# RWKV attention and a gated MLP on one core: decay, k and r packed into three blocks of 128 features, with heads 6 and 7 gathered by moves inside SBUF

## The chip, the core and the metric

The kernel runs on one core of one Trainium2 chip. The core has a matrix engine (PE, with its weight loads on PEld), three engines for vectors (DVE, ACT, POOL), and queues that issue DMAs; in the kernel before, all of them go out from the queue of the Sync engine (SPq). The metric is device time in microseconds of one launch. "Span" is the time from the first to the last instruction in a profiled execution.

## The reference, cut to what matters

Four sequences, 8 heads, 768 tokens, 48 features per head. First a linear attention with a decay per feature, then a gated MLP whose gate mixes the tokens:

```python
for t in range(S):                                   # S = 768, per (b, h), D = 48
    cur = np.einsum('bhd,bhe->bhde', u[None] * kt, vt)
    y[:, :, t] = np.einsum('bhd,bhde->bhe', rt, state + cur)
    state = wt[:, :, :, None] * state + np.einsum('bhd,bhe->bhde', kt, vt)
...
h = gelu(x @ w_in)                                   # x is y as (b, t, 384); d_ff = 1024
u, v = h[..., :512], h[..., 512:]
v_n = (v - mu) / np.sqrt(var + 1e-06) * g_ln
v_s = np.einsum('ts,bsd->btd', w_sg, v_n) + b_sg[None, :, None]
out = x + (u * v_s) @ w_out
```

## The kernel before

**Tiling.** The 768 tokens of a sequence are six chunks of 128 (`C`), so there are 24 chunks. In a chunk the decays are turned into running products, and the attention becomes matmuls: the scores of the chunk's own tokens (`scores`, L486), the product with the state that the earlier chunks left (`outputs`, L548), the product of the masked scores with v (L563), and the update of the state (`state`: transposes of k, L500, and k with v, L510). The MLP works on halves of a sequence (three chunks): `v_piece` per chunk, then four `u_piece`, four `gate_piece` and three `out_piece` per half. Every MLP product is three matmuls (L632, L633, L634), since both operands are split in a high and a low part.

**Layout of decay, k and r.** Eight heads of 48 features lie in four blocks (`NP`), two heads per block: one in partitions 0 to 47, one in 64 to 111. Partitions 48 to 63 and 112 to 127 are padding. So a tile of w, k or r is 128 partitions by 4 x 128 tokens (512 columns).

**Per chunk.** `decays` scans w backwards (L408, 516 columns) and forwards (L413); L415 and L436 multiply r and k by the results; `range_check` (L424) squares the products for a check of their size; `chunk_pc` copies the four last columns into a tile of its own, by which `decayed` scales the state (L531 on ACT, L533 elsewhere). `own_weights` makes the weight of each token for itself: in the first 8 chunks (`OWN_PE`) r times k (L446) and four matmuls with `u_col` (L450), later from a second copy of k and r, laid out by tokens (L458, L460, L463). L471 or L473 puts these weights on a diagonal, and L490 copies the scores in below it.

**What sets the order.** [...] Each piece of work is a generator that yields `Op`s with a cost for each engine that may run it, what they come after, and which buffers they take and free. `Plan.run` plays all generators against these costs and ranks and picks engine and place, so each engine and the DMA queue get a fixed order. The ranks come from tables of numbers (`LEAD`, `FIRST`, `PIECE`, `WEIGHT`). An engine works its list in order, and waits at the first instruction whose inputs aren't there.

**Weights.** `f64_weight` loads a weight matrix as 64-bit numbers and makes a high and a low part: four DVE instructions (L761, L763, L766, L768), one on ACT (L785), three matmuls (L772 to L774). The six blocks of `w_in` must be ready before the first `v_piece` and `u_piece`. Three of them use buffers of `vn`, three those of `xT`.

**Moves.** Heads 3 and 7 leave `outputs` in a tile of their own and are put into the padding of x by six small DMAs per chunk or half (`move`, L600).

## Time and profile before

| | us |
|---|---|
| median of 3 runs | 404.07 (403.16 to 404.13) |
| the profiled execution's own time | 402.04 |
| its span | 400.3 |
| PE busy | 378.3 (95% of the span) |
| DVE busy | 294.2 (73%) |
| ACT busy | 200.2 (50%) |
| POOL busy | 94.2 (24%) |

A busy time is the union of an engine's instructions. A row of a group gives line, engine, operation, the tile written and the tiles read, shapes and count, then busy time and mean duration, then the idle time in front and what ended it. A row of a timeline gives start, duration, engine, line, operation and count. A row of a table of stages gives, for each stage, its length and each engine's busy time (with the number of instructions), the clock granted to PE and the share of the DMA engines.

### The profile page before, as it was taken

The page shows a single profiled execution, that of the slowest core. Times are in us where ns is not written, and L with a number is a line of the kernel's source. Part 1 is how long each engine was busy: PE and PEld are TensorE (multiplying, and loading weights), DVE is VectorE, ACT ScalarE, POOL GpSimd, SP SyncE. Part 2 cuts the span into 40 slices and gives each one's busy share as a digit, 9 for nine tenths or more (in the row PEclk, how much of TensorE's full clock was granted, in tenths as well). Part 3 has the DMA queues.
Part 4 walks back from the last instruction along what each step waited for, and adds up shares of the span by engine and source line. Part 5 has one row for each costly group of instructions (what it writes and reads, how often), then busy time and mean ns, then how long its engine had stood idle before and what let it go on. Part 6 is the DMA issues. An engine that isn't in the chain of part 4 may idle for free. (4 is left out here: it accounts for less than half of the span.)

```text
span 400.3 us, 7881 instructions
## 1 busy us (share of the span) xinstructions
PE 378.3 (95%) x2964; PEld 329.8 (82%) x2964; DVE 294.2 (73%) x573; ACT 200.2 (50%) x534; POOL 94.2 (24%) x127
## 2 busy tenths in 40 slices
PE   2799889999999999999999999999999999999993
PEld 2666567889898988988899988979899789999993
DVE  7699989889989999998798489956653355543251
ACT  3566575685555447746454246563272576502010
POOL 3003551123073543444550003124100002100000
PEclk9999899999999999999999999999999999999999
DMA  8918667343134634335422316222133520100101
GB/s 281 355 42 250 188 220 241 129 135 105 46 131 160 221 118 144 98 122 196 155 88 77 105 65 211 60 88 96 61 106 111 186 95 2 39 22 0 61 0 66
DMA packets 23933, 48.82 MB, mean 122 GB/s; under 512 B 4048, under 2 KB 13008, under 8 KB 23888
## 3 DMA queue, kind: packets, MB, share of 16 engines
q1 hardware_dynamic: 23888, 48.25, 36.6%
q8 instruction: 25, 0.41, 0.4%
q14 instruction: 20, 0.16, 0.1%
HBM read 42.34 MB, written 4.72 MB: 118 GB/s over the span
## 5 line engine op out<-in xcount | busy, mean ns | idle before, releaser
L632 PE MATMUL m_ps<-wsgh,vn 128*128 128x384 f32 x192 | 67.7, 353 | 0.8 <-DVE g L714 0.8
L634 PE MATMUL m_ps<-wsgh,vn 128*128 128x384 f32 x192 | 64.7, 337 | 0.0
L633 PE MATMUL m_ps<-wsgl,vn 128*128 128x384 f32 x192 | 64.6, 337 | 0.0
L473 POOL TENSOR_SCALAR_AFFINE_SELECT a<-own 128x512 f32<-128x512 f32 x25 | 20.3, 815 | 94.9 <-PE y_ps L563 44.9
L632 PEld LDWEIGHTS m_ps<-wsgh,vn 128*128 128x128 f32 x192 | 36.1, 188 | 5.5 <-issue 2.9
L712 ACT CAST g<-m_ps 128x384 fp32r<-128x384 f32 x32 | 15.1, 479 | 50.1 <-DVE m_ps L710 50.0
L490 DVE COPY_PREDICATED a<-mask,a_ps 128x512 f32<-128x512 uint8 x48 | 34.4, 730 | 4.5 <-POOL a L473 2.5
L663 POOL TENSOR_TENSOR st<-st,mhalf 128x1 f32<-128x1 f32 x24 | 15.3, 640 | 90.9 <-DVE st L661 87.7
L633 PEld LDWEIGHTS m_ps<-wsgl,vn 128*128 128x128 f32 x192 | 36.2, 188 | 0.4
L634 PEld LDWEIGHTS m_ps<-wsgh,vn 128*128 128x128 f32 x192 | 36.1, 188 | 0.0
L708 DVE SCALAR_TENSOR_TENSOR m_ps<-m_ps,g_ln,b_bc 128x384 f32<-128x384 f32 x32 | 19.7, 622 | 21.5 <-PE m_ps L634 21.4
L632 PE MATMUL m_ps<-g,wouth 128*128 128x384 f32 x96 | 33.7, 351 | 0.4 <-DVE g L714 0.4
L632 PE MATMUL m_ps<-xT,winh 128*128 128x384 f32 x96 | 33.4, 348 | 0.0
L408 DVE TENSOR_TENSOR_SCAN W<-W,D 128x516 f32<-128x516 f32 x24 | 32.0, 1332 | 1.6 <-DMA W<-in_wpad 1.6
L634 PE MATMUL m_ps<-xT,winl 128*128 128x384 f32 x96 | 32.4, 337 | 0.0
L633 PE MATMUL m_ps<-xT,winh 128*128 128x384 f32 x96 | 32.4, 337 | 0.0
L633 PE MATMUL m_ps<-g,wouth 128*128 128x384 f32 x96 | 32.4, 337 | 0.0
L634 PE MATMUL m_ps<-g,woutl 128*128 128x384 f32 x96 | 32.4, 337 | 0.0
L413 DVE TENSOR_TENSOR_SCAN W<-W,D 128x516 f32<-128x516 f32 x24 | 31.4, 1308 | 0.1
L471 ACT ACTIVATE a<-ident,own 128x128 f32<-128x128 f32 x92 | 29.1, 393 | 3.9 <-DVE own L463 3.8
L632 PE MATMUL m_ps<-winh,xT 128*128 128x512 f32 x72 | 30.5, 424 | 0.0
L424 ACT ACTIVATE junk<-W 128x1032 f32<-128x1032 f32 x24 | 25.6, 1066 | 9.8 <-DVE W L413 6.8
(142 smaller groups left out, 856.5 us busy)
## 6 DMA issues: line engine op xcount, KB each, us to landing
KR<-in_kr SPq DMA_DIRECT2D x24, 512.0 KB, 3.5
W<-in_wpad SPq DMA_DIRECT2D x24, 258.5 KB, 2.9
RK<-in_ktok SPq DMA_DIRECT2D x16, 384.0 KB, 3.2
vtok<-in_vtok SPq DMA_DIRECT2D x24, 192.0 KB, 3.1
out<-o SPq DMA_DIRECT2D x24, 192.0 KB, 1.9
KR<-in_w_in SPq DMA_DIRECT2D x6, 512.0 KB, 4.1
u<-in_w_sgT SPq DMA_DIRECT2D x12, 192.0 KB, 3.6
vn<-in_w_in SPq DMA_DIRECT2D x3, 512.0 KB, 7.3
```

Of the source, the lines that this page charges most:

```text
L408: nc.vector.tensor_tensor_scan(Suf[:, WL - 1:0:-1], W[:, WL - 1:0:-1], D1[:, WL - 1:0:-1], 0.0, ALU.mult, ALU.add)
L413: nc.vector.tensor_tensor_scan(W[:, 0:WL - 1], W[:, 0:WL - 1], D2[:, 0:WL - 1], 0.0, ALU.mult, ALU.add)
L424: nc.scalar.activation(junk.rearrange("p (a x) -> p a x", a=2), both, AF.Square, accum_out=chk[:, n:n + 1])
L471: nc.scalar.activation(a[:, p], ident, AF.Copy, scale=own.tile[:, 2 * p + j:2 * p + j + 1])
L473: nc.gpsimd.affine_select(a, own.tile[:, j:H:2].unsqueeze(2).broadcast_to([128, NP, C]), pattern=[[0, NP], [1, C]], compare_op=ALU.is_equa ...
L490: nc.vector.copy_predicated(x.a[j].tile, mask, a_ps.tile[j])
L632: nc.tensor.matmul(ps, lh, rh, start=(i == 0), stop=False)
L633: nc.tensor.matmul(ps, lh, rl, start=False, stop=False)
L634: nc.tensor.matmul(ps, ll, rh, start=False, stop=(i == n - 1))
L663: nc.gpsimd.tensor_tensor(rstd, var, c.mhalf, ALU.pow)
L708: nc.vector.scalar_tensor_tensor(ps, ps, c.g[:, d:d + 1], c.b_bc[:, ts], ALU.mult, ALU.add)
L712: nc.scalar.copy(gh, ps)
```

## The change

**Layout.** w, k and r of all eight heads are packed into three blocks (`NB`) of 128 full partitions. Heads 0 to 5 keep their 48 partitions in each half of a block; heads 6 and 7 are cut into three pieces of 16 features, which fill partitions 48 to 63 and 112 to 127. Loads, scans, multiplications and the check so run over three quarters of the columns, and the transposes and the matmuls with `u_col` are three instead of four. For the scores and the product with the state, heads 6 and 7 are needed in a block of their own: `gather` moves them, after the multiplications, by six DMAs per chunk from the padding rows of the three blocks to a fourth block of the same tile. The copy of the last decays now lies in that tile and moves along. Matmuls on k and r read 48 partitions per head instead of 64. The copy of the transposed k (`kt`) becomes three copies that sort the heads.

**Order.** The planner gets a later time for an `Op` that takes several buffers, lets the two diagonals, the three copies of y and the small DMAs be ordered apart from each other, can issue moves from SPq or from ACT's queue, charges PE for turning from large to small matmuls, and has new ranks. The `w_in` blocks all go through buffers of `vn` and wait for less. `u_col` is laid out by the caller and loaded in one DMA. The weights for the own token come from PE in the first 5 chunks instead of 8. KR has four buffers instead of three.

**Order on PE up to the first piece of the MLP.** PE's rows just before the first `v_piece`, which starts at L632. `KR_0_82` is chunk 3 here, the x tile's block is that of chunk 0. Before:

```order
L563 MATMUL y_ps_1_129<-a_0_97,vtok_0_87 64x128 x4
L772 MATMUL m_ps_0_131<-xT_367,ident 128x512
...
L548 MATMUL y_ps_1_129<-KR_0_82,S_0_103 64x128
L500 MATMUL k_ps_0_127<-ident,KR_0_82 128x128 x4
L486 MATMUL a_ps_0_125<-KR_0_82 128x128
...
L621 MATMUL m_ps_0_132<-x_0_105,ident 128x384
L622 MATMUL m_ps_0_132<-xT_506,minus 128x384
L510 MATMUL k_ps_0_127<-vtok_0_85,kt_0_100 64x48 x8
L450 MATMUL m_ps_0_130<-u_col,RK_0_89 128x8 x4
L632 MATMUL m_ps_0_131<-winh,xT_506 128x512
```

With the change (L534 is the transposes, L548 k with v, L601 the masked scores with v, L663 the split of x, L674 the first MLP matmul; `KR_0_84` is chunk 2):

```order
L586 MATMUL y_ps_1_126<-KR_0_83,S_0_100 64x128
L534 MATMUL k_ps_0_124<-ident,KR_0_84 128x128 x3
L601 MATMUL y_ps_0_125<-a_0_95,vtok_0_87 64x128 x4
L601 MATMUL y_ps_1_126<-a_0_96,vtok_0_87 64x128 x4
L548 MATMUL k_ps_0_124<-vtok_0_88,kt_0_97 64x48 x8
L808 MATMUL m_ps_0_128<-vn_253,ident 128x512
...
L663 MATMUL m_ps_0_129<-x_0_102,ident 128x384
L664 MATMUL m_ps_0_129<-xT_416,minus 128x384
L808 MATMUL m_ps_0_127<-vn_277,ident 128x512
...
L674 MATMUL m_ps_0_128<-winh,xT_416 128x512
```

The first `v_piece` stood behind the scores of chunk 3; it now stands ahead of the scores of chunk 2, right behind the last block of `w_in`.

**Order on the DMA queue of SP.** The loads of the weights, before (`vn` and `xT` take `w_in`, the third and later rows of KR and W are chunks 2 and on):

```order
L384 DMA KR_0_84<-in_kr 128x1024
L392 DMA vtok_0_87<-in_vtok 128x384
L756 DMA vn_173<-in_w_in 128x1024
L756 DMA vn_177<-in_w_in 128x1024
L812 DMA u_col<-in_u 48x4x1
L756 DMA vn_183<-in_w_in 128x1024
```

and with the change, from the first loads to the first gathers (L469, the other half of whose rows go out from ACT's queue):

```order
L847 DMA u_col<-in_ucol 128x24
L399 DMA W_0_81<-in_wpad 128x388
L407 DMA KR_0_83<-in_kr 128x3x256
L415 DMA vtok_0_86<-in_vtok 128x384
L791 DMA vn_170<-in_w_in 128x1024
...
L407 DMA KR_0_85<-in_kr 128x3x256
L469 DMA KR_0_82<-KR_0_82 16x256 x3
L399 DMA W_0_80<-in_wpad 128x388
L791 DMA vn_241<-in_w_in 128x1024
```

The first `w_in` block now comes after the loads of two chunks instead of three, and three gathers of chunk 0 stand ahead of the third load of W. In the whole program 91 of the 144 gathers and 49 of the 72 moves of y are issued by SP, 53 and 23 by ACT.

The core of the diff:

```diff
...
+NB = KT
 Q = C + 1
-WL = NP * Q + 1
+WL = NB * Q + 1
+KW = 2 * C + 4
...
-LEAD = (2.78, 2.05, 2.47, 2.9)
-FIRST = {"v": -1.57, "u": 4.03, "gate": 5.24, "out": 7.56}
-PIECE = {"v": -0.45, "u": 3.56, "gate": 5.0, "out": 7.56}
-WEIGHT = {"v": -8.15, "u": -9.0, "sg0": 4.48, "sg1": 3.78, "out": 4.95, "g": -1.62}
-
-OWN_PE = 8
-COLD = 20.0
+LEAD = (2.81, 2.14, 2.13, 2.02)
+FIRST = {"v": -1.35, "u": 4.47, "gate": 2.25, "out": 7.29}
+PIECE = {"v": -0.3, "u": 4.01, "gate": 4.96, "out": 7.68}
+WEIGHT = {"v": -4.16, "u": -2.73, "sg0": 2.61, "sg1": -1.74, "out": 3.69, "g": 0.54}
+
+BIAS = {"DVE": 0.05, "POOL": 0.05}
+MOVE = {"SP": 0.53, "ACT": 0.55}
+
+ON_PE = {"own": 5, "x": 6, "w": 6}
+FIRST_LOADS = {(0, "load_w"): -20.0, (0, "load_kr"): -19.0, (1, "load_w"): -17.0, (1, "load_kr"): -16.0,
+               (0, "load_v"): -15.0}
+COLD = 15.0
...
-    def since(self):
-        return min(t for t, _ in self.free)
+    def since(self, n):
+        return sorted(t for t, _ in self.free)[n - 1]
...
+    def cost(self, op, e, t):
+
+        c = op.on[e]
+        if e == "PE":
+            c = (2 * c if t < COLD else c) + (0.09 if op.small and not self.small else 0.0)
+        return c
...
-            p[2] = op.seen
+            if not op.apart:
+                p[2] = op.seen
...
-    s_w = slots("W", 2, [2 * 521])
-    s_kr = slots("KR", 3, [2, NP * C])
+    s_w = slots("W", 2, [2 * 393])
+    s_kr = slots("KR", 4, [NP, KW])
...
-    nc.gpsimd.memset(u_col, 0.0)
     for _, t in s_S2.free:
+        nc.gpsimd.memset(t, 0.0)
+    for _, t in s_kr.free:
+        nc.gpsimd.memset(t[:, NB], 0.0)
+    for _, t in s_kt.free:
         nc.gpsimd.memset(t, 0.0)
...
+    def move_dma(kb, after):
+        return Op(MOVE, kb=kb, after=after, apart=True)
...
-        ch[n].W, ch[n].Suf = (ch[n].w.tile[:, i * 520:(i + 1) * 520] for i in range(2))
+        ch[n].W, ch[n].Suf = (ch[n].w.tile[:, i * 392:i * 392 + 390] for i in range(2))
...
+        nc.sync.dma_start(ch[n].KR[:, 0:NB, 0:2 * C], kr[b, g])
...
-        yield Op({"DVE": 1.15}, after=[x.e_W], done=x.e_suf, two=True)
+        yield Op({"DVE": 0.88}, after=[x.e_W], done=x.e_suf, two=True)
...
-        yield Op({"DVE": 1.15}, done=x.e_pre, two=True)
+        yield Op({"DVE": 0.88}, done=x.e_pre, two=True)
         nc.vector.tensor_tensor_scan(W[:, 0:WL - 1], W[:, 0:WL - 1], D2[:, 0:WL - 1], 0.0, ALU.mult, ALU.add)
-        op = yield Op({"DVE": 0.61, "POOL": 1.25}, after=[x.e_KR, *x.own], done=x.e_r, two=True)
-        engine[op.e].tensor_tensor(cols(x.KR[:, 1]), cols(x.KR[:, 1]), blocks(W, 0), ALU.mult)
+        op = yield Op({"DVE": 0.48, "POOL": 1.05}, after=[x.e_KR, *x.own], done=x.e_r, two=True)
+        r = x.KR[:, 0:NB, C:2 * C]
+        engine[op.e].tensor_tensor(r, r, blocks(W, 0), ALU.mult)
...
+        copy(op.e, x.KR[:, 0:NB, 2 * C], x.Suf[:, 1:WL - 1:Q])
...
+        op = yield Op({"DVE": 0.48, "POOL": 1.05}, after=[x.e_KR, x.e_suf, *x.own], done=x.e_k, two=True)
+        k = x.KR[:, 0:NB, 0:C]
+        engine[op.e].tensor_tensor(k, k, blocks(x.Suf, 2), ALU.mult)
...
+    def gather(n):
+
+        x = ch[n]
+        w = 2 * C + (steps[n][1] > 0)
+        for j in range(2):
+            for i in range(NB):
+                op = yield move_dma(16, [x.e_k, x.e_r, *([x.e_pc] if steps[n][1] else [])])
+                issue[op.e].dma_start(x.KR[64 * j + 16 * i:64 * j + 16 * i + 16, NB, 0:w],
+                                      x.KR[64 * j + D:64 * j + 64, i, 0:w])
+        x.e_km.t = op.seen
...
-            op = yield Op({"DVE": 0.6, "POOL": 1.25}, after=[x.e_KR], take=[s_rk], done=x.e_own, two=True)
...
-            t = rk.tile.rearrange("p a b -> p (a b)")[:, 0:NP * C]
-            engine[op.e].tensor_tensor(t, x.KR[:, 0], x.KR[:, 1], ALU.mult)
-            op = yield Op({"PE": 0.35}, after=[e_uc], take=[m_m], free=[rk])
+            t = rk.tile[:, 0].rearrange("p (b t) -> p b t", t=C)
+            engine[op.e].tensor_tensor(t, x.KR[:, 0:NB, 0:C], x.KR[:, 0:NB, C:2 * C], ALU.mult)
+            op = yield Op({"PE": 0.75}, small=True, after=[e_uc], take=[m_m], free=[rk])
             m, = op.got
-            for p in range(NP):
-                nc.tensor.matmul(m.tile[:, 0:H], t[:, p * C:(p + 1) * C], u_col[:, p], start=(p == 0),
-                                 stop=(p == NP - 1))
+            for i in range(NB):
+                nc.tensor.matmul(m.tile[:, 0:H], t[:, i], u_col[:, i], start=(i == 0), stop=(i == NB - 1))
...
         for j in range(2):
-            op = yield Op({"POOL": 0.95, "ACT": 1.2}, take=[s_a], done=(x.e_A0, x.e_A1)[j], free=[own] if j else [])
+            op = yield Op({"POOL": 0.95, "ACT": 1.2}, take=[s_a], done=(x.e_A0, x.e_A1)[j], free=[own], apart=True)
...
-        op = yield Op({"PE": 1.09}, after=[x.e_k, x.e_r], take=[m_a])
+        op = yield Op({"PE": 1.06}, small=True, after=[x.e_km], take=[m_a])
...
-                nc.tensor.matmul(a_ps.tile[j][:, p], x.KR[64 * j:64 * j + 64, 0, p * C:(p + 1) * C],
-                                 x.KR[64 * j:64 * j + 64, 1, p * C:(p + 1) * C], start=True, stop=True)
+                nc.tensor.matmul(a_ps.tile[j][:, p], x.KR[64 * j:64 * j + D, p, 0:C],
+                                 x.KR[64 * j:64 * j + D, p, C:2 * C], start=True, stop=True)
...
-        for p in range(NP):
-            nc.tensor.transpose(kt_ps.tile[:, p], x.KR[:, 0, p * C:(p + 1) * C], ident)
-        op = yield Op({"ACT": 0.5, "DVE": 0.61}, take=[s_kt], free=[kt_ps])
+        for i in range(NB):
+            nc.tensor.transpose(kt_ps.tile[:, i], x.KR[:, i, 0:C], ident)
+        op = yield Op({"ACT": 0.72, "DVE": 0.7}, take=[s_kt], free=[kt_ps])
         kt, = op.got
-        copy(op.e, kt.tile, kt_ps.tile)
-        op = yield Op({"PE": 0.6}, after=[x.e_V], take=[m_s], free=[kt])
+        halves_ = lambda t: t.rearrange("p b (j x) -> p b j x", x=64)
+        copy(op.e, halves_(kt.tile[:, 0:NB])[:, :, :, 0:D], halves_(kt_ps.tile[:, 0:NB])[:, :, :, 0:D])
+        for j in range(2):
+            copy(op.e, kt.tile[:, NB, 64 * j:64 * j + D].rearrange("p (i e) -> p i e", e=16),
+                 kt_ps.tile[:, 0:NB, 64 * j + D:64 * j + 64])
+        op = yield Op({"PE": 0.6}, small=True, after=[x.e_V], take=[m_s], free=[kt])
...
-        op = yield Op({"DVE": 0.3, "POOL": 0.6, "ACT": 1.0}, after=[before.e_S1, x.e_pc], take=[s_S2], done=x.e_S2,
+        op = yield Op({"DVE": 0.3, "POOL": 0.6, "ACT": 1.0}, after=[before.e_S1, x.e_km], take=[s_S2], done=x.e_S2,
...
             engine[op.e].tensor_tensor(x.S2.tile[:, :, 0:D], before.S1.tile,
-                                       x.pc.tile.unsqueeze(2).broadcast_to([128, NP, D]), ALU.mult)
+                                       x.KR[:, :, 2 * C:2 * C + 1].broadcast_to([128, NP, D]), ALU.mult)
         before.S1.done(op.seen)
-        x.pc.done(op.seen)
+        x.kr.done(op.seen)
...
-                nc.tensor.matmul(y.tile[j][64 * c_:64 * c_ + 64, q, 0:C], x.S2.tile[64 * j:64 * j + 64, p],
-                                 x.KR[64 * j:64 * j + 64, 1, p * C:(p + 1) * C], start=(q == 0), stop=False,
+                nc.tensor.matmul(y.tile[j][64 * c_:64 * c_ + 64, q, 0:C], x.S2.tile[64 * j:64 * j + D, p],
+                                 x.KR[64 * j:64 * j + D, p, C:2 * C], start=(q == 0), stop=False,
...
-                op = yield dma(10, after=[ch[h_.n + g].e_y for g in range(g0, g1)])
+                op = yield move_dma(10, [ch[h_.n + g].e_y for g in range(g0, g1)])
                 x, y3 = h_.x.tile, h_.y3.tile
-                nc.sync.dma_start(x[64 * j + D:64 * j + 64, i, ts], y3[64 * j + 16 * i:64 * j + 16 * i + 16, ts])
+                issue[op.e].dma_start(x[64 * j + D:64 * j + 64, i, ts], y3[64 * j + 16 * i:64 * j + 16 * i + 16, ts])
...
-        for j in range(2):
-            op = yield dma(1)
-            nc.sync.dma_start(u_col.rearrange("p a b -> p (a b)")[64 * j:64 * j + D, j:NP * H:10],
-                              u.rearrange("(p j) d -> j d p", j=2)[j])
-        e_uc.t = op.seen
+        yield dma(16, done=e_uc)
+        nc.sync.dma_start(u_col, ucol)
...
-            plan.add(r, f64_weight(*w[1:], e_win[n0][k], r, [s_vn, s_vn] if n0 else [s_xt],
-                                   [ch[0].e_KR] if n0 else [ch[1].e_k]))
...
-_INS = ["wpad", "kr", "vtok", "ktok", "vt", "u", "w_in", "g_ln", "w_sgT", "b_sg", "w_out"]
+KROWS = [h * D + e for i in range(NB) for j in range(2)
+         for h, e0, n in ((2 * i + j, 0, D), (6 + j, 16 * i, 16)) for e in range(e0, e0 + n)]
...
+    cut = lambda a: a.transpose(0, 1, 3, 2).reshape(B, DM, NC, C)[:, KROWS].reshape(B, NB, 128, NC, C).transpose(
+        0, 3, 2, 1, 4)
+    wpad = np.zeros((B, NC, 128, WL), np.float32)
+    wpad[..., 0:NB * Q].reshape(B, NC, 128, NB, Q)[..., 1:] = cut(w)
+    kr = np.stack([cut(k), cut(r)], axis=4)
+
+    ucol = np.zeros((DM, H), np.float32)
+    for h in range(H):
+        ucol[h * D:(h + 1) * D, h] = u[h]
...
```

More of the change, by code (lines that the diff above doesn't have):

```diff
@@ L427, in chunk_pc @@
         x = ch[n]
[L428 to L429 removed]
+        op = yield Op({"ACT": 0.13, "POOL": 0.38}, after=[x.e_suf, x.e_KR], done=x.e_pc)
         x.w.done(op.seen)
[L431 removed]
+        copy(op.e, x.KR[:, 0:NB, 2 * C], x.Suf[:, 1:WL - 1:Q])
     def decayed_k(n):
         x = ch[n]
[L435 removed]
@@ L572, in outputs @@
         copy(op.e, half.y3.tile[:, cs], y1[:, 1])
[L573 to L579 removed]
+        x.e_y.t = max(seen, op.seen)
     halves = {}
```

163 lines of the change are left out of this document (78 added, 85 removed).

## The prediction

> **What bounds the kernel now.** The page first: who is busy, and when.
>
> ```profile
> span 400.3 us, 7881 instructions
> ...
> PE 378.3 (95%) x2964; PEld 329.8 (82%) x2964; DVE 294.2 (73%) x573; ACT 200.2 (50%) x534; POOL 94.2 (24%) x127
> ...
> PE   2799889999999999999999999999999999999993
> ...
> DVE  7699989889989999998798489956653355543251
> ```
>
> PE is busy 378.3 of 400.3 us, so 22.0 are to be had from its idle time, and the rest only by taking work off it. The slices show two stages: an early one in which PE has gaps and DVE is as full as PE, and a long one in which PE is full. The table of stages separates them:
>
> ```profile
> 0.00:10.00 10.00, 2.93 (x27) 2.46 (x29) 7.31 (x13) 3.68 (x8) 3.14 (x19) 1.00 0.80 282
> 10.00:20.00 10.00, 7.64 (x33) 6.15 (x32) 6.48 (x13) 5.90 (x19) 0.64 (x1) 1.00 0.91 355
> 20.00:40.00 20.00, 18.88 (x195) 13.22 (x194) 20.00 (x36) 13.56 (x41) 3.64 (x4) 1.00 0.48 146
> 40.00:49.50 9.50, 7.53 (x66) 5.23 (x64) 9.50 (x14) 4.94 (x16) 5.36 (x5) 0.82 0.59 187
> 49.50:80.00 30.50, 28.75 (x264) 22.44 (x264) 26.45 (x53) 20.14 (x54) 8.39 (x13) 1.00 0.62 196
> 80.00:320.00 240.00, 239.13 (x1987) 209.90 (x1986) 189.25 (x372) 126.58 (x338) 68.46 (x77) 1.00 0.37 120
> ...
> 380.00:400.30 20.30, 13.43 (x76) 12.79 (x74) 7.64 (x14) 1.92 (x4) 0.00 (x0) 0.97 0.10 33
> ```
>
> Up to 49.5, where the first `v_piece` starts, PE is idle for 12.5 us (7.07 + 2.36 + 1.12 + 1.97), and DVE has no gap from 20 on: there DVE and the loads set the pace. From 49.5 to 380 PE is idle for 2.6 (1.75 + 0.87), and 6.9 are the tail. What PE waited for:
>
> ```profile
> PE k_ps L500 <- DVE KR L436: 6.4, 1, 6.4
> PE m_ps L450 <- DMA u_col<-in_u: 2.4, 1, 2.4
> PE y_ps L548 <- ACT S L531: 2.0, 1, 2.0
> ```
>
> The first two are the start and the late `u_col`; the third is one gap at 40.8. Behind that gap PE also runs slowly:
>
> ```profile
> 24.21 0.66 PE L500 MATMUL k_ps<-ident,KR 128*128 128x128 f32 x4
> 24.80 1.16 PE L486 MATMUL a_ps<-KR 64*128 64x128 f32 x16
> 25.89 1.06 PE L450 MATMUL m_ps<-u_col,RK 128*128 128x8 f32 x8
> 26.88 0.67 PE L510 MATMUL k_ps<-vtok,kt 128*64 128x48 f32 x16
> 27.48 0.67 PE L548 MATMUL y_ps<-KR,S 64*64 64x128 f32 x16
> ...
> 42.74 1.11 PE L548 MATMUL y_ps<-KR,S 64*64 64x128 f32 x16 [1.96 <-ACT S L531]
> ...
> 44.51 2.08 PE L486 MATMUL a_ps<-KR 64*128 64x128 f32 x16
> ...
> 50.43 1.09 PE L563 MATMUL y_ps<-a,vtok 128*64 128x128 f32 x16
> ```
>
> The scores take 2.08 us instead of 1.16, the product with the state 1.11 instead of 0.67; the granted clock of that stage is 0.82, so 0.18 x 9.5 = 1.7 us of PE time are lost beside the 2.0 of the gap. The Trainium skill ("TensorE: Matmul & The Clock Gate", Part 1) has PE at half clock until some 3.4 us of sustained work; 1.7 us lost at half clock are 3.4 us, so the trace agrees. It also warns only of idle gaps over about 3.4 us, while here a gap of 2.0 was enough; by the page a short new wait would cost its own length alone, by the trace about twice that.
>
> **The change, part by part.** I sum up to the first MLP matmul and from there on.
>
> *DVE before the first `v_piece`.* The forms of DVE up to 39.6 and its busy time from its first scan to the end of the last `w_in` conversion:
>
> ```profile
> L413 DVE TENSOR_TENSOR_SCAN W<-W,D 128x516 f32<-128x516 f32 x4 | 4.9, 1226 | 0.0
> L490 DVE COPY_PREDICATED a<-mask,a_ps 128x512 f32<-128x512 uint8 x6 | 4.3, 722 | 2.5 <-POOL a L473 2.5
> L446 DVE TENSOR_TENSOR RK<-KR 128x512 f32<-128x512 f32 x5 | 3.7, 745 | 0.0
> L436 DVE TENSOR_TENSOR KR<-KR,W 128x512 f32<-128x512 f32 x3 | 2.0, 680 | 0.0
> L761 DVE TENSOR_SCALAR vn<-vn 128x512 int32<-128x512 int32 x3 | 1.3, 423 | 1.0 <-DMA vn<-in_w_in 1.0
> ```
> ```profile
> 3.68:39.51 35.83, 28.97 (x249) 21.64 (x250) 32.31 (x57) 21.37 (x62) 4.39 (x6) 1.00 0.69 240
> ```
>
> DVE needs 32.3 us for its list up to there, and idles 3.5. In the new list scans go from seven to six and to three quarters of the columns (7 x 1.23 to 6 x 0.92: -3.1), the products for the own token from five to two (3.7 to 1.1: -2.6), the k and r products from five to four (3.4 to 2.0: -1.4), the masked copies from six to four (-1.4); an added kt copy in three pieces, three small copies and one cast, less small ones, come to about +1.4 (an estimate by columns). That leaves 25.2. From 3.7 it ends at 28.9 without a wait and at 32.4 with the 3.5 us of before. I take 30: with the sizes of the issue rows below, cut by a quarter for W and KR, the first `w_in` block has landed after 1.9 MB instead of 3.1, which at the 355 GB/s of stage 10 to 20 is 3.5 us earlier.
>
> *PE before the first `v_piece`.* Two pieces of work that weren't shown yet, a block of `w_in` (39.20 to 40.79, 1.6 us) and the split of x (56.83 to 57.92, 1.1 us):
>
> ```profile
> 39.20 1.13 PE L772 MATMUL m_ps<-xT,ident 128*128 128x512 f32 x2
> ...
> 40.40 0.39 PE L774 MATMUL m_ps<-winl,same 128*128 128x512 f32 x1
> ...
> 56.83 0.91 PE L621 MATMUL m_ps<-x,ident 128*128 128x384 f32 x2 [0.98 <-DMA x<-y]
> 57.37 0.55 PE L622 MATMUL m_ps<-xT,minus 128*128 128x384 f32 x1
> ```
>
> The third `w_in` block is converted after 13 us of DVE's list (by the same durations), at 17, and the scores of chunk 0 stand behind it on PE. From there to L674 PE has two scores, two own (three quarters of 1.06), two transposes (three quarters of 0.66), two k with v, one state and two masked products, three blocks of `w_in` and one split: 2.3 + 1.6 + 1.0 + 1.3 + 0.7 + 2.2 + 4.8 + 1.1, with 1 us for the slow clock at their start and 1.5 for turns between kinds (estimates) 17.5. So **34.5**, later than DVE's 30; not below 32 (nothing waits and the clock is up), not above 40 (before's two DVE waits and one gap with its slow clock).
>
> *The rest.* Before:
>
> ```profile
> 49.50:400.30 350.80, 341.31 (x2651) 302.74 (x2650) 250.86 (x501) 172.15 (x455) 81.43 (x98) 1.00 0.33 108
> 49.50:400.30 350.80, 2.10 (x18) 2.20 (x17) 1.00 0.33 108
> 49.50:400.30 350.80, 9.75 (x64) 7.72 (x64) 1.00 0.33 108
> ```
>
> PE has 341.3 us of work there, 2.1 of it L450 and 9.75 L500 (second and third row). The new order leaves work of chunks 2 and 3 for later that was done by 49.5: two scores, two state and one masked product, one k with v, 2.3 + 1.3 + 1.1 + 0.7 = 5.4, and one group of transposes, 0.5. The transposes are three instead of four: a quarter of 17 x 0.61, -2.6 (between 0.42 and 0.66 us per group by PEld and PE: -1.8 to -2.8). Own: two groups of three, 1.6 instead of 2.1. So 344.1.
>
> *Gathers.* No row shows one; the nearest are the six moves of y, of the same 16 partitions:
>
> ```profile
> 40.02 0.51 SPq L600 DMA_DIRECT2D x<-y  x1
> ...
> KR<-in_kr SPq DMA_DIRECT2D x24, 512.0 KB, 3.5
> W<-in_wpad SPq DMA_DIRECT2D x24, 258.5 KB, 2.9
> ...
> vtok<-in_vtok SPq DMA_DIRECT2D x24, 192.0 KB, 3.1
> ...
> vn<-in_w_in SPq DMA_DIRECT2D x3, 512.0 KB, 7.3
> x<-y SPq DMA_DIRECT2D x36, 8.0 KB, 3.1
> ```
>
> Three issues on a queue and the landing: 1.5 + 3.1 = 4.6 us from the last product to the scores, 6.2 where one queue issues all. The Trainium skill ("DMA: Bandwidth & Descriptors", Anatomy of one DMA) gives about 2.0 us of fixed cost, by which it were 3.5 us; the row decides. The wait stands in front of PE's scores, and behind them on PE all MLP work. I cost it at nothing after chunk 1, since DVE's list runs a chunk ahead of PE and MLP matmuls stand between; without that cover it is 4.6 per chunk. On SP the loads of W and RK are queued behind gathers, three or more issues of 0.5 each; these loads are a chunk early. On ACT 76 issues of 0.5, 39 us, fit beside its 200. The third wait of before (L531 on ACT) goes mostly: four such instructions are left of 40.
>
> *Idle after the start.* 2.6 before; I take 3: chunks 2 to 5 now run beside MLP work, which covers PE, but have less lead. Below: 0.5. Above: 12, three gaps like that at 40.8 with their slow clock (3.7 each). Tail: 6.9, the last matmuls are in the same order.
>
> *Sum.* 34.5 + 344.1 + 3 + 6.9 = 388.5 of span, 11.8 less than 400.3. The profiled execution's own time is 402.04, 2.0 under the median of 404.07; I take the difference from the median: **392.3**.
>
> **The rivals.**
>
> 1. *PE never waits.* v at 32, 0.5 idle: 383.5, so 387.3. For it: DVE's list is 7 us shorter, and stage 80 to 320 has 0.9 us of gaps. Against: PE gets to the scores by way of DVE, DMA and DVE again. Chance 0.25.
> 2. *DVE stays the bound up to chunk 5.* It has the masked copies, weights of `w_sg` and the first v pieces at once; PE reaches them earlier than DVE. v at 36 and 9 us of gaps: 396, so 399.8. For it: DVE 26.45 of 30.5 from 49.5 to 80. Chance 0.15.
> 3. *The gathers take the place of the waits, slower.* 24 chunks each wait for six small DMAs in front of the scores. It decides from 11.8 / 24 = 0.5 us uncovered per chunk; with 0.8 it is 388.5 + 19.2 = 407.7 of span, 411.5. For it: 4.6 us where there were 0.2. Against: the lead of about a chunk. Chance 0.08.
> 4. *Matmuls on 48 partitions don't run in pairs.* Pairs show in eight state products at 0.67 us, while four transposes take 0.66. Without them 0.65 x 20 more, 405.3. The Trainium skill ("TensorEngine Tiling (Array Packing)", When to Use Tiling) has a contraction of up to 64 in the 64-row mode; no run here shows 48. Chance 0.01.
> 5. *It gives all back.* 404, no difference: 0.03.
>
> **How the numbers follow.** The forecast has 0.48. Its own range is 386 to 399. The range for 8 in 10 takes in rival 1 and most of rival 2: 384 to 401. A difference under 0.3%, 1.2 us, can't be told from none. Faster: 0.48 + 0.25 + 0.15 = 0.88; same 0.03; slower 0.09.
>
> **What would show it.** The first MLP matmul (L674) near 34.5; PE busy under 374; the waits of PE with L520 on DMA KR at nearly nothing; no stage after 20 us with a granted clock under 0.95; scores at 1.16 per 16. Wrong: L674 after 40, a wait of L520 for KR of more than 5 us in all, or PE busy above 378.

## The result, and the profile after

The changed kernel takes **417.97 us** (median of 4 runs, 415.15 to 419.01) beside 403.62 for the kernel before (402.79 to 404.13): a ratio of 1.035, with a 95% interval of 1.029 to 1.040. It is slower. Forecast were 392.3.

The page of the changed kernel, its busy times, two engines and the clock in 40 slices, and the chain of waits by engine:

```profile
span 415.7 us, 8089 instructions
...
PE 383.6 (92%) x2910; PEld 333.9 (80%) x2910; DVE 279.8 (67%) x608; ACT 185.9 (45%) x505; POOL 88.8 (21%) x135
...
PE   2879869899999599997999999999999999999993
...
PEclk9969967999999779997999999999999999999998
...
PE 69%; DMA 11%; DVE 9%; SPq 4%; ACT 3%; issue 2%; POOL 1%; ACTq 1%; DVEq 0%; POOLq 0%
```

DVE and ACT have less to do, as the layout promised, and so has PE (2910 matmuls instead of 2964); yet PE is busy for 383.6 us, 5.3 more than before. The slices say why: at several places up to the middle of the run PE has a gap and, in the same slice or the next, a lower granted clock (the digits 5 to 8 of `PE`, 6 and 7 of `PEclk`). In the chain DMA has 11% and SPq 4%. (Before, DMA had 1%, but there the chain is followed through only a fifth of the span.)

The table of stages, cut where the first `v_piece` starts (L674, at 37.65), at 200, and at the tail:

```profile
0.00:37.60 37.60, 25.82 (x182) 18.25 (x183) 29.11 (x59) 17.26 (x48) 11.91 (x32) 0.91 0.73 234
37.60:200.00 162.40, 148.84 (x1191) 125.31 (x1191) 130.28 (x281) 83.48 (x233) 52.41 (x65) 0.91 0.44 136
200.00:395.40 195.40, 195.40 (x1468) 177.82 (x1468) 112.75 (x256) 83.23 (x222) 24.46 (x38) 1.00 0.26 82
395.40:415.70 20.30, 13.50 (x74) 12.54 (x72) 7.68 (x14) 1.93 (x4) 0.00 (x0) 0.94 0.10 34
```

The start did get shorter: L674 comes at 37.65 instead of 49.55. All of that and more is given back between 37.6 and 200, where PE idles for 13.6 us (162.40 - 148.84) at a mean clock of 0.91; from 200 on it never waits until the tail. What it waited for in that stretch (total, times, longest):

```profile
PE m_ps L674 <- DVE g L756: 4.2, 1, 4.2
PE k_ps L548 <- ACT kt L283: 3.0, 1, 3.0
PE y_ps L601 <- DVE st L703: 2.8, 1, 2.8
PE k_ps L534 <- DVE st L699: 2.0, 1, 2.0
PE m_ps L663 <- ACT v L697: 1.3, 1, 1.3
```

No row has PE waiting for a gather (`DMA KR<-KR`): the scores (L520) find their fourth block there. The five gaps lie in front of other work, and no two have the same name. Two that follow each other closely, of 2.0 and 2.8 us, followed back. First SP's queue, then the chain of waits, then PE, then DVE:

```profile
43.84 3.37 SPq L469 DMA_DIRECT2D KR<-KR  x5
47.38 0.46 SPq L399 DMA_DIRECT2D W<-in_wpad  x1
47.94 0.61 SPq L407 DMA_DIRECT2D KR<-in_kr  x1
48.60 1.18 SPq L838 DMA_DIRECT2D u<-in_w_sgT  x2
```
```profile
48.60 4.71 DMA u<-in_w_sgT
...
53.33 0.51 ACT wsgh L283
...
54.39 0.56 DVE wsgl L842
54.95 0.92 DVE vn L716
55.87 0.64 DVE a L524
```
```profile
49.83 0.67 PE L586 MATMUL y_ps<-KR,S 48*64 48x128 f32 x16
52.51 0.52 PE L534 MATMUL k_ps<-ident,KR 128*128 128x128 f32 x3 [2.01 <-DVE st L699]
53.12 0.66 PE L601 MATMUL y_ps<-a,vtok 128*64 128x128 f32 x8
56.56 1.12 PE L601 MATMUL y_ps<-a,vtok 128*64 128x128 f32 x8 [2.79 <-DVE st L703]
...
60.34 2.08 PE L520 MATMUL a_ps<-KR 48*128 48x128 f32 x16
```
```profile
48.84 0.36 DVE L571 TENSOR_TENSOR S<-S,KR 128x192 f32<-128x192 f32 x1 [1.74 <-DMA KR<-KR]
...
50.22 1.23 DVE L430 TENSOR_TENSOR_SCAN W<-W,D 128x387 f32<-128x387 f32 x1 [0.95 <-DMA W<-in_wpad]
...
52.01 0.35 DVE L558 TENSOR_TENSOR S<-k_ps,S 128x192 f32<-128x192 f32 x1
```

Five gathers hold SP for 3.4 us; the loads of W, KR and `w_sgT` (the weights that mix the tokens) stand behind them. The gap of 2.8 comes from `w_sgT`: it lands at 53.3; ACT's conversion, next in its list, has waited for it, and DVE's list waits for ACT; the masked copy (L524) is last of all. The gap of 2.0 in front of the transposes (L534) has ended before that. They write the one `k_ps` tile, which L558 has to read first, and DVE is late with L558 because its list has waited 1.74 us for a gather's landing (L571 scales the state by the moved decays) and 0.95 us for W, whose load stood behind the five gathers. After both gaps the scores take 2.08 us instead of 1.16. The gap of 3.0, which ends at 192.28, goes back to SP as well: from 170.1 to 179.4 SP issues four moves and eight gathers, with two loads between them; the RK load behind them goes out at 180.1 and lands at 185.1, and DVE's list and then ACT's copy of kt come late by it. The experiments ask whether the gathers do this, or the order, and by what.

### The profile page after: what moved, and what is told of

The parts are those of the page before. It is cut to its first block, busy times and chain, and to the rows that moved or that the text cites. A ratio compares the mean times of both kernels' runs of the same rounds, so it can differ in the third digit from the quotient of the medians.

```text
span 415.7 us, 8089 instructions
## 1 busy us (share of the span) xinstructions
PE 383.6 (92%) x2910; PEld 333.9 (80%) x2910; DVE 279.8 (67%) x608; ACT 185.9 (45%) x505; POOL 88.8 (21%) x135
## 4 chain that ended last, share of the span: by engine, by line
PE 69%; DMA 11%; DVE 9%; SPq 4%; ACT 3%; issue 2%; POOL 1%; ACTq 1%; DVEq 0%; POOLq 0%
PE m_ps L674 19%; PE m_ps L675 17%; PE m_ps L676 17%; PE a_ps L520 5%; PE y_ps L601 4%; DMA RK<-in_ktok 2%; PE k_ps L548 2%; DMA KR<-in_kr 2%; DMA x<-y 2%; DMA vn<-in_w_in 2%; PE y_ps L586 2%; SPq L469 2%; DMA u<-in_w_sgT 1%; PE k_ps L534 1%; DVE W L430 1%
## 5 line engine op out<-in xcount | busy, mean ns | idle before, releaser
L674 PE MATMUL m_ps<-wsgh,vn 128*128 128x384 f32 x192 | 70.7, 368 | 4.3 <-DVE g L756 4.2
L675 PE MATMUL m_ps<-wsgl,vn 128*128 128x384 f32 x192 | 66.8, 348 | 0.0
L676 PE MATMUL m_ps<-wsgh,vn 128*128 128x384 f32 x192 | 66.5, 346 | 0.0
L674 PEld LDWEIGHTS m_ps<-wsgh,vn 128*128 128x128 f32 x192 | 37.5, 195 | 9.4 <-DVE g L756 4.9
L754 ACT CAST g<-m_ps 128x384 fp32r<-128x384 f32 x32 | 15.3, 483 | 54.9 <-DVE m_ps L752 53.3
L675 PEld LDWEIGHTS m_ps<-wsgl,vn 128*128 128x128 f32 x192 | 37.7, 196 | 0.4
L676 PEld LDWEIGHTS m_ps<-wsgh,vn 128*128 128x128 f32 x192 | 37.5, 195 | 0.0
L524 DVE COPY_PREDICATED a<-mask,a_ps 128x512 f32<-128x512 uint8 x48 | 34.2, 726 | 3.8 <-PE a_ps L520 3.8
L674 PE MATMUL m_ps<-xT,winh 128*128 128x384 f32 x96 | 34.2, 356 | 0.0
L674 PE MATMUL m_ps<-g,wouth 128*128 128x384 f32 x96 | 33.3, 347 | 0.4 <-DVE g L756 0.4
L520 PEld LDWEIGHTS a_ps<-KR 48*128 48x128 f32 x384 | 25.7, 204 | 6.5 <-issue 6.0
L674 PE MATMUL m_ps<-winh,xT 128*128 128x512 f32 x72 | 30.8, 428 | 0.0
L601 PE MATMUL y_ps<-a,vtok 128*64 128x128 f32 x384 | 28.2, 290 | 2.9 <-DVE st L703 2.8
L520 PE MATMUL a_ps<-KR 48*128 48x128 f32 x384 | 30.6, 304 | 0.0
L447 ACT ACTIVATE junk<-W 128x774 f32<-128x774 f32 x24 | 20.4, 852 | 22.8 <-DVE W L435 16.1
```

The costliest lines, as they stand in the source:

```text
L447: nc.scalar.activation(junk.rearrange("p (a x) -> p a x", a=2), both, AF.Square, accum_out=chk[:, n:n + 1])
L520: nc.tensor.matmul(a_ps.tile[j][:, p], x.KR[64 * j:64 * j + D, p, 0:C], x.KR[64 * j:64 * j + D, p, C:2 * C], start=True, stop=True)
L524: nc.vector.copy_predicated(x.a[j].tile, mask, a_ps.tile[j])
L601: nc.tensor.matmul(y.tile[j][64 * c_:64 * c_ + 64, q, 0:C], x.V[:, h * D:h * D + 64], x.a[j].tile[:, p], start=(g == 0 and q == 0), stop=( ...
L674: nc.tensor.matmul(ps, lh, rh, start=(i == 0), stop=False)
L675: nc.tensor.matmul(ps, lh, rl, start=False, stop=False)
```

## The experiments

Theory A: the gathers cost by being issued, in queues that work in order. Theory B: the new order makes the gaps. Theory C: the way from the products through the gathers to the scores is too long. The kernel before, run beside each group of experiments, took 403.0 to 404.1 us; a ratio is always to the runs beside it.

### What the gathers cost (e1, e2, e3, e4)

**e1**, the gathers left out, the order of all else kept (heads 6 and 7 are missing from its result):

```diff
-                issue[op.e].dma_start(x.KR[64 * j + 16 * i:64 * j + 16 * i + 16, NB, 0:w],
-                                      x.KR[64 * j + D:64 * j + 64, i, 0:w])
```

> The order of the changed kernel on every engine, but the 144 gathers are not issued (the fourth block stays zero, so heads 6 and 7 are left out of the result; every other instruction is there). Theory A (the gathers, issued in order by SP and ACT, hold up the loads and the ACT work behind them): 388 to 400 us, PE idle under 25 us, granted clock 0.98 or more. Theory B (the new order itself, with its small lead of the chunks, makes the gaps, whatever the gathers do): 412 to 420 us, the same gaps between 50 and 200 us. Theory C (the landing time of a gather in front of scores and decayed state is what PE waits for) expects what A expects here; the next run tells A from C.

**397.41 us** (395.16 to 398.45), ratio 0.985 (0.980 to 0.990): the gathers cost 20.6 us. Its stages, cut at its first `v_piece`, at 180 and at the tail:

```profile
0.00:38.50 38.50, 26.30 (x183) 18.45 (x184) 28.87 (x60) 18.10 (x49) 12.79 (x32) 0.87 0.70 223
38.50:180.00 141.50, 136.68 (x1189) 116.65 (x1188) 127.49 (x277) 82.62 (x232) 52.96 (x65) 0.99 0.47 146
180.00:376.10 196.10, 196.10 (x1471) 178.44 (x1470) 114.50 (x260) 83.72 (x224) 23.51 (x39) 1.00 0.26 78
376.10:396.40 20.30, 13.20 (x72) 12.23 (x71) 7.36 (x14) 1.92 (x4) 0.00 (x0) 0.96 0.10 34
```

From the first `v_piece` on, the same matmuls keep PE busy for 346.0 us (136.68 + 196.10 + 13.20) and for 357.7 with gathers (148.84 + 195.40 + 13.50): 11.8 us are slow clock. Before the tail PE idles for 4.8 instead of 13.6: 8.7 us are waits. The changed kernel has 0.9 less at the start and 0.3 less idle time in the tail, and that is the whole difference of the spans, 19.3.

The slow clock can be seen directly. These are the stretches in which the granted clock was 0.50: all three of the changed kernel between the first `v_piece` and the tail, the one of e1 there, and the one of the kernel before behind its gap at 40.8:

```profile
54.70:68.35 13.65, 11.79 (x74) 8.30 (x76) 9.33 (x20) 4.65 (x12) 3.23 (x5) 0.50 0.61 189
140.05:150.25 10.20, 9.23 (x39) 8.47 (x40) 8.44 (x16) 3.61 (x13) 4.66 (x4) 0.50 0.31 90
191.25:198.05 6.80, 5.77 (x43) 5.35 (x44) 6.39 (x16) 3.09 (x11) 3.36 (x3) 0.50 0.30 99
```
```profile
74.00:77.35 3.35, 3.35 (x9) 2.41 (x8) 3.35 (x7) 2.41 (x6) 0.73 (x1) 0.50 0.31 79
```
```profile
44.20:47.55 3.35, 3.35 (x22) 2.52 (x19) 3.35 (x4) 1.09 (x3) 2.24 (x2) 0.50 0.44 90
```

In the changed kernel PE works 26.8 us at half clock (11.79 + 9.23 + 5.77), of which about half, 13.4, is lost; in e1 it is 1.7. The difference, 11.7, is nearly all of the 11.8. A gap of 2.0 us (before) or 2.2 (e1) was followed by 3.4 us of slow clock, one of 3.0 by 6.8, one of 4.2 by 10.2, and the pair of 2.0 and 2.8 by 13.6.

**e2**, the same order and the full result, but two DMAs a chunk in place of six, each from 16 partitions of three blocks to 48 partitions (the copy of kt follows the new order of the rows):

```diff
+            issue[op.e].dma_start(x.KR[64 * j:64 * j + D, NB, 0:w],
+                                  x.KR[64 * j + D:64 * j + 64, 0:NB, 0:w])
```

> The same order again and the whole result, but the six gathers of a chunk go out as two DMAs of 48 rows each, at the place of the third and the sixth; the rows of the fourth block are then in the order (feature, block), and the kt copy follows. 96 issues less on SP and ACT, the landing in front of the scores stays. Theory A: a good part of the loss comes back, 395 to 408 us, with RK and w_sgT loads issued earlier than in the changed kernel. Theory C: no gain, 414 to 421 us. Theory B: 412 to 420 us.

**400.52 us** (399.51 to 401.28), ratio 0.993 (0.990 to 0.996): 17.4 of the 20.6 us come back. The views of the gathers' line in the changed kernel and in e2 give their landings (least, median, most):

```profile
DMA to landing us min/median/max: 1.7/2.2/6.2
```
```profile
DMA to landing us min/median/max: 2.1/2.5/7.4
```

A gather of e2 lands later, not sooner, so it isn't the landing of the single DMA that costs. The way to the scores has become shorter by issues all the same, so e2 alone doesn't rule out theory C.

**e3** is e2 with the planner making an order of its own:

> Two gathers a chunk as in the run before, but the planner knows of it and makes its own order. Theory A: 392 to 406 us. Theory B: the order is much like that of the changed kernel, so the gaps stay: 410 to 420 us. Theory C: 412 to 420 us.

**416.88 us** (415.61 to 419.02). The same DMAs and the same work in another order: 16.4 us. Theory A alone doesn't account for this.

**e4**, the order alone: the layout of before (`NB = NP`, scans of 516 columns, four blocks, three KR buffers, no gathers) with the new rules and ranks.

> The new planner's rules, ranks and u in columns loaded whole, but the layout of before: four blocks of 128 rows with 48 of each 64 in use, scans of 516 columns, no gathers at all. Theory A: no loss, 392 to 404 us (about 8 us of DVE work and 3 us of PE work more than the changed kernel, no held-up loads). Theory B: slower than before, 410 to 422 us, with gaps and slow clock between 50 and 200 us. Theory C: as A.

**415.81 us** (415.19 to 416.43), ratio 1.032 (1.028 to 1.035). So there are two effects: the gathers, 20.6 us in one order, and the order.

### Which order (e5, e7, e11, e12, e14, e15)

The expectations split theory B: B1, the new ranks do the harm; B2, the new rules of the planner do.

**e5**: e4 with the four tables of ranks of before. **e7**: e3 with two ranks of before:

```diff
-WEIGHT = {..., "sg0": 2.61, "sg1": -1.74, ...}
+WEIGHT = {..., "sg0": 4.48, "sg1": 3.78, ...}
```

> As the run of the order alone (layout of before, no gathers, new planner's rules, u in columns loaded whole), but LEAD, FIRST, PIECE and WEIGHT have the numbers of before. Theory B1 (the new ranks, above all w_sgT at 2.61 and -1.74 instead of 4.48 and 3.78, put weight conversions that wait for their loads at the head of ACT's and DVE's lists): 398 to 406 us. Theory B2 (the rules themselves, with the true dependencies, thin out the lead whatever the ranks): 410 to 420 us. Theory A says nothing here, there are no gathers.

> Two gathers a chunk in the planner's own order (416.9 us), with only the ranks of the w_sgT weights as before (4.48 and 3.78). Theory B1: 396 to 408 us. Theory B2: 412 to 420 us.

**e5: 420.15 us** (2 runs), **e7: 402.31** (400.33 to 403.58). By e7 the ranks of the `w_sgT` weights are worth 14.6 us; by e5 the old ranks don't help. **e11** is e4 with the two ranks of e7; **e12** is e7 with the moves of y as two DMAs as well:

> The order alone (layout of before, no gathers, 415.8 us) with only the w_sgT ranks of before (4.48 and 3.78). Theory B1 (these ranks cost what the order alone costs, as with two gathers, where they gave 14.6 us): 398 to 406 us. Theory B2 (the rules): 412 to 420 us.

> Two DMAs a chunk for the gathers, two for each set of moves, the planner's own order with the w_sgT ranks of before. Theories A and B1 together: at most the 402.3 us of the same without the two-DMA moves, and as good as 397.1 us of the order of the changed kernel with both: 393 to 402 us. Theory B2: 405 to 418 us.

**e11: 420.51 us** (2 runs), **e12: 407.30** (403.62 to 408.23), both against B1: ranks that gain in one kernel lose in another, and fewer DMAs in an order made anew can be slower. B2 had 412 to 420 us for e11 and 405 to 418 for e12. Against it stands theory D: any order that the planner makes anew loses 10 to 15 us against one that was measured on the chip. So the last two take the kernel before, with its old rules, and only nudge it: **e14** three ranks of weights by at most 0.18, **e15** the leads by at most a fifth of a chunk.

```diff
-WEIGHT = {"v": -8.15, "u": -9.0, "sg0": 4.48, "sg1": 3.78, "out": 4.95, "g": -1.62}
+WEIGHT = {"v": -8.15, "u": -9.0, "sg0": 4.3, "sg1": 3.6, "out": 4.8, "g": -1.62}
```
```diff
-LEAD = (2.78, 2.05, 2.47, 2.9)
+LEAD = (2.6, 2.2, 2.3, 2.7)
```

> The kernel before with three ranks of its planner moved a little: sg0 4.48 to 4.30, sg1 3.78 to 3.60, out 4.95 to 4.80; nothing else. Theory D (any order that the planner makes anew loses some 10 to 15 us against one that was measured on the chip, since its costs do not know the chip's waits; the order alone lost its 12 us in this way): 410 to 420 us. Theory B2 (it is the new rules that lose): 401 to 407 us.

> The kernel before with LEAD 2.60, 2.20, 2.30, 2.70 instead of 2.78, 2.05, 2.47, 2.90, nothing else. Theory D: 408 to 420 us. Theory B2: 401 to 408 us, the leads are moved by less than a fifth of a chunk.

**e14: 415.97 us** (2 runs), ratio 1.032 (1.021 to 1.044); **e15: 405.40** (403.35 to 406.45), ratio 1.003 (0.999 to 1.008). A nudge of ranks with no change of rules, layout or work can lose 12 us, nearly as much as e4; another loses nothing that can be seen, which D had not expected (408 to 420). So e4, e5 and e11 don't show that the new rules are worse, only that an order of this planner carries some 10 to 17 us of luck, time that the planner's costs don't foresee. Whether the rules are better or worse on the mean stays open. What the changed kernel loses is not this: in its own order, without gathers, it takes 1.5% less than before (e1), and with few of them no more than before (e2).

### How the gathers cost it (e6, e8, e9, e10, e13)

These five keep the changed kernel's order. **e8** lets ACT issue all gathers (`nc.scalar` for `issue[op.e]`), **e10** POOL (`nc.gpsimd`):

> The order of the changed kernel with its six gathers a chunk, but all 144 issued by ACT at their place in the program: 91 issues less on SP, 91 more on ACT. If it is SP's queue that does the harm (loads of RK, W, KR and w_sgT behind gathers): 398 to 408 us. If it is the time that ACT gives to the issues and to waiting for the products in front of them: 418 to 440 us. If both alike: 412 to 420 us.

> The order of the changed kernel with six gathers a chunk, but POOL issues all of them at their place: SP has 91 issues less and ACT 53 less, and POOL, busy for 89 of 416 us, has 144 more. If it is what stands behind a gather in SP's and ACT's lists that counts, 398 to 410 us, or somewhat more where POOL's own products wait behind gathers (its `a` matrices stand in front of the masked copies); if a gather costs the same wherever it is issued, 415 to 425 us.

**e8: 424.10 us** (2 runs), **e10: 413.95** (2 runs). Neither is near 400: no queue takes them for free. On ACT they cost more than on both queues, as expected if ACT's time does the harm (418 to 440); on POOL the time lies between the two cases that were expected (398 to 410, 415 to 425). On POOL each issue takes 0.48 us of its working time, 144 of them 69.7, and its busy time goes from 88.8 to 156.3.

**e9** splits every gather in two of 8 rows, twelve a chunk, the same bytes. **e13** leaves the six as they are and adds six DMAs of 16 times 4 bytes behind them, to a tile that nobody reads, so that no scores need them:

```diff
+                for o in (0, 8):
+                    r0, r1 = 64 * j + 16 * i + o, 64 * j + D + o
+                    issue[op.e].dma_start(x.KR[r0:r0 + 8, NB, 0:w], x.KR[r1:r1 + 8, i, 0:w])
```
```diff
+        for q, e in enumerate(on):
+            issue[e].dma_start(dz[0:16, 6 * n + q:6 * n + q + 1], ident[0:16, 0:1])
```

> The order of the changed kernel, but every gather goes out as two DMAs of 8 rows, so twelve a chunk, each pair at the place of the one: 144 issues more on SP and ACT, the same bytes. Theory A (issues in the two in-order queues): taking away 96 gave 17 us and taking away all 144 gave 20, so adding 144 costs 15 to 40 us: 433 to 458 us. Theory C (the landing of the last gather of a chunk): only three more issues on the path of a chunk, 418 to 424 us.

> The order of the changed kernel with its six gathers a chunk, and behind the sixth six more DMAs of 16 times 4 bytes from a constant to a tile that nobody reads, on the queues of the six: 144 issues more, no bytes to speak of, nothing more in front of this chunk's scores. Theory A in its second form (each issue takes its 0.5 us and one of the eight DMA semaphores that all queues share in turn, so that the eighth DMA before it must have landed; computing instructions of ACT and loads of SP stand behind that): nearly the cost of the twelve gathers, 440 to 465 us, and ACT's waits for landings it does not need far above the changed kernel's. Theory C (the way from the products through the gathers to the scores got too long): 418 to 426 us.

**e9: 462.46 us** (2 runs), ratio 1.145 (1.138 to 1.152). **e13: 455.49** (2 runs), ratio 1.131 (1.116 to 1.146). 144 DMAs that carry 9 KB in all and that nothing needs cost 37.5 us. So theory C isn't needed for most of it: of the 44.5 us that e9 costs, e13 costs 37.5. Some of it is there: the scores of e9 wait 7.8 us for gathers, and in the changed kernel DVE and POOL wait 9.6 us in all for gathers in front of L571. Over 0, 48, 144 and 288 gathers the times are 397, 401, 418 and 462: the price of one grows, from 0.06 over 0.18 to 0.31 us.

An issue takes 0.58 us on SP (91 of them) and 0.59 on ACT (53) in the changed kernel, and 0.59 and 0.60 for the 64 bytes of e13. SP's rows (least, median, most, in ns):

```profile
L469 SPq DMA_DIRECT2D KR<-KR x91: 507/581/1408, 13.8 to 291.0; - x91
...
```
```profile
L475 SPq DMA_DIRECT2D dz<-ident x91: 507/587/1312, 17.2 to 329.6; - x91
...
```

That is one part. The other shows in the list of SP's program in e13, three gathers of a chunk and its tiny DMAs, with what each waits for:

```
L471 DMA KR_0_82<-KR_0_82 16x256 [waits DMAHW0_49,DVE_49,Pool_49]
...
L471 DMA KR_0_82<-KR_0_82 16x256 [waits DMAHW4_49]
L475 DMA dz<-ident 16x1 [waits DMAHW6_49,Pool_49]
L475 DMA dz<-ident 16x1 [waits DMAHW7_49]
L475 DMA dz<-ident 16x1 [waits DMAHW0_49]
```

The tiny DMAs need no data, and still 137 of the 144 wait in the program for a DMA semaphore. The program has eight, `DMAHW0` to `DMAHW7`, which the DMAs of SP and ACT take in turn: before one can be used again, the DMA that had it must have landed. Every small DMA so ties a queue to the landing of one some places before it, a load or another gather, and what stands behind in SP's or ACT's list, loads or computing, waits too. ACT's waits in e13 show it: the cast of a weight (L826), the two `gelu` of the MLP (L702, L735) and a cast of the gate (L759), which use neither `dz` nor KR, have stood behind them:

```profile
ACT winh L826 <- DMA KR<-KR: 7.6, 1, 7.6
...
ACT g L759 <- DMA dz<-ident: 5.0, 1, 5.0
ACT v L702 <- DMA KR<-KR: 4.6, 1, 4.6
ACT u L735 <- DMA dz<-ident: 4.3, 1, 4.3
```

The waits of SP and ACT that end with a DMA's landing, summed over all rows, are 29 us without gathers (e1), 40 in e2, 61 in the changed kernel, 105 in e8, 107 in e9 and 114 in e13 (some are true needs, as `w_sgT` above). One such place on ACT, in the changed kernel and in e1:

```profile
29.44 2.39 ACTq L642 DMA_DIRECT2D x<-y  x2
31.88 0.63 ACT L821 CAST winh<-vn 128x512 fp32r<-128x512 f32 x1 [3.09 <-DMA u<-in_w_sgT]
```
```profile
28.39 0.60 ACTq L640 DMA_DIRECT2D x<-y  x1
...
29.03 0.62 ACT L819 CAST winh<-vn 128x512 fp32r<-128x512 f32 x1 [0.46 <-issue]
```

In the changed kernel ACT does nothing for 3.1 us and then casts a weight that has nothing to do with y or `w_sgT`. In front of the cast stands the second of two moves of y, and in the program that move waits for a semaphore which a load of `w_sgT` had last. SP starts these loads at 25.58, behind three gathers, and at 21.32 in e1, where ACT waits 0.5 us. The first piece of the MLP is no later for this one (37.6, in e1 38.5); it shows the way, not the price. How much of the 20.6 us is issue time, how much the semaphores and how much the landings in front of L571 wasn't separated.

**e6** therefore cuts the issues further: e2, with the six moves of y as two DMAs as well, and the features of heads 3 and 7 in the order that this needs:

```diff
+            issue[op.e].dma_start(h_.x.tile[64 * j + D:64 * j + 64, :, ts], h_.y3.tile[64 * j:64 * j + D, ts])
...
-        for h, e0, n in ((HEADS[i][j], 0, D), (REST[j], 16 * i, 16)) for e in range(e0, e0 + n)]
+        for h, es in ((HEADS[i][j], range(D)), (REST[j], range(i, D, KT))) for e in es]
```

> The order of the changed kernel, two DMAs a chunk for the gathers as before in the run with the same order, and the six moves of y also as two DMAs of 48 rows (the feature order of heads 3 and 7 in x and in the weights' rows follows). 48 issues less on SP and ACT. Theory A: another 1 to 5 us less than 400.5, so 395 to 400 us, since moves stand in the same queues in front of loads. Theory C (landing times count, not the issues): no change, 400 to 402 us.

**397.09 us** (396.30 to 398.47), ratio 0.984 (0.979 to 0.989). The same piece of SP's queue as above: two gather issues instead of five, and every load 3.5 us earlier:

```profile
42.37 1.31 SPq L469 DMA_DIRECT2D KR<-KR  x2
43.77 0.53 SPq L399 DMA_DIRECT2D W<-in_wpad  x1
44.40 0.61 SPq L407 DMA_DIRECT2D KR<-in_kr  x1
45.06 1.07 SPq L837 DMA_DIRECT2D u<-in_w_sgT  x2
```

PE's same place has one gap of 1.32 us instead of 2.01 and 2.79, and the scores keep to 1.16:

```profile
53.10 0.66 PE L601 MATMUL y_ps<-a,vtok 128*64 128x128 f32 x8 [1.32 <-DVE st L702]
...
55.15 1.16 PE L520 MATMUL a_ps<-KR 48*128 48x128 f32 x16
```

### The version with few DMAs again (e16, e17, e18)

**e16** and **e17** are the kernel of e6 again (e16's label is that of an idea which e18 tries). **e18** is the same with SP issuing all gathers and moves (`nc.sync` for `issue[op.e]`).

> Withdrawn in favour of the run e6, of which this is a repetition: 396 to 399 us by every theory.

> The kernel of e6 once more (two DMAs a chunk for the gathers, two for each set of moves, the order of the changed kernel), with more rounds: the single execution of e16, which was this kernel too, took 401.9 us where e6 had 396.3 to 398.5. If e6 stands, 396 to 399 us and a ratio of 0.980 to 0.990; if not, 399 to 402 us and a ratio of 0.990 to 0.997.

> The same kernel, but SP issues all gathers and all moves, so that no computing instruction of ACT stands behind a DMA that waits for a semaphore: 50 to 60 of the 96 small DMAs are on SP already. Theory A in its second form: ACT's waits for landings shrink, SP has about 20 us more of issues: 394 to 399 us. If the loads behind them on SP count as much as ACT's work: 397 to 404 us.

**e16: 401.93 us** in a single execution. **e17: 394.92** (392.01 to 397.04, 6 runs), ratio 0.977 (0.972 to 0.982). **e18: 393.78** (392.52 to 395.28), ratio 0.976 (0.970 to 0.982). The version with few DMAs was 1.6% faster than the kernel before in e6, 2.3% in e17, 2.4% as e18 and 0.5% in the single execution of e16, which is outside the 396 to 399 us expected of it; why that one was slower stays open. It is 5 to 6% faster than the changed kernel, by e6, e17 and e18; e18's waits for landings (24 us on SP and ACT together) are not fewer than e17's (18), and the two can't be told apart.

## Why the prediction was wrong

**The step that failed: "I cost it at nothing after chunk 1".** The gathers were priced about right as a wait in front of the scores, 4.6 us, hidden by the lead of a chunk: PE never waits there. What was put at nothing is what the 144 issues do to what stands *behind* them, and the second place that needs a landing, the scaling of the state (L571), for which DVE and POOL wait 9.6 us. The first of the two the prediction named, "on SP the loads of W and RK are queued behind gathers", and closed with "these loads are a chunk early"; the loads of `w_sgT`, which have no such lead, it didn't name. On ACT "76 issues of 0.5, 39 us, fit beside its 200" weighs busy time against busy time; but ACT works its list in order, and an issue that waits stops the computing behind it. Measured: 20.6 us in this order (e1), 0.86 a chunk, of the 25.7 between forecast and result.

**Without that term the other steps stay within their bounds.** Their misses still add up to 7.9 us: e1 gains 5.6 us on the kernel before, where 11.8 were forecast. Against e1, by the prediction's own steps:

| step | predicted | e1 | changed kernel |
|---|---|---|---|
| first L674 | 34.5 | 38.5 | 37.6 |
| PE's work after it | 344.1 | 346.0 | 357.7 |
| idle after it | 3 | 4.8 | 13.6 |
| tail | 6.9 | 7.1 | 6.8 |
| span | 388.5 | 396.4 | 415.7 |

**First L674.** Within its bounds (32 to 40), 3.1 late: the scores of chunk 0 start at 19.1, where 17 was taken, and from there it is 18.6 us instead of 17.5. The stage from 20 to 40 has a clock of 0.83, in e1 0.74, where 1 us had been set aside for all of the slow clock at the start. The gathers aren't the cause: in e1 the first L674 is later still.

**PE's work.** "PE busy under 374" came out at 372.3 in e1 and 383.6 in the changed kernel: the transposes, the matmuls with `u_col` and the rest were costed right, and 11.8 us of slow clock came on top. Of the 1.9 us by which e1 exceeds the forecast, 1.7 are its own slow clock.

**Idle.** Its upper bound, 12 us for three gaps, was passed, with 13.6, and the 12 held the slow clock already, at 1.7 us for a gap of 2.0; measured are 11.8 us for 8.7 of idle time, so the slow clock behind a gap was priced too low as well: 3.4 us of half clock were taken for each, and the longer gaps brought 6.8, 10.2 and 13.6. That a gap of 2.0 is enough for the slow clock the prediction read from the trace against the Trainium skill ("TensorE: Matmul & The Clock Gate", Part 1). The gap of 2.2 in e1 bears it out. The gap of 2.0 at 52.51 by itself doesn't: the transposes behind it take 0.52 us, and the clock falls at 54.7, in the second gap; what the first gap added can't be told. Behind the gap of 1.3 at 79.28 the clock stayed at 1.00.

**The rivals.** Rival 3, at 0.08, has the right sign, the right culprit and, at 411.5, a time 6.5 us short of the measured one, but not the place: it had PE waiting in front of the scores. Rival 4 is false: scores on 48 partitions take 1.16 us per 16, as on 64. Rival 2 is false: from 37.6 to 80 DVE is busy for 30.6 of 42.4 us, and in e1, where it is busy for 18.4 of the 20 us from 40 to 60, PE idles for 1.3. Rival 1 would have been 387.3; the best version with the gathers in few DMAs has 393.8.

**The signs.** "The waits of PE with L520 on DMA KR at nearly nothing" held and meant nothing. "No stage after 20 us with a granted clock under 0.95" and "PE busy above 378" showed the failure.

## What to carry to other kernels

A small DMA isn't priced by its landing alone: count its issue on an engine that works in order, and whatever stands behind it there, loads and computing, and count how many DMAs may be under way at once. Where several small moves have one source and one destination, put the features in an order that lets one DMA do them: here two for six gave back 17 of 21 us in one and the same order. The Trainium skill ("DMA: Bandwidth & Descriptors", Rules for kernel authors) says to coalesce small transfers, and that spreading them over the queues saves issue time only; e2 agrees with the first (17.4 us), and e8 and e10 show that another queue is no way out (+6 and -4 us). And where a planner makes the order, compare within one order: a nudge of its ranks moved 12 us, more than most edits.
